# Two products between a snapshot and the next use of its bank, half of the output-weight casts on ScalarE, and three more weight sums in image 0

## The chip, the cores and the metric

The kernel runs on one core of a Trainium2 chip. The time is the device time of one execution in microseconds (us). The kernel before takes 420.86 us (median of 3 runs, 420.32 to 421.15). A result is called faster or slower when it differs by over 2%. Engines: TensorE (PE), VectorE (DVE), ScalarE (ACT), GpSimd (POOL); SyncE (SP) starts the transfers.

## The reference, cut to what matters

```python
# attention with a sigmoid, 8 images x 12 heads x 448 tokens x 64
scores = q @ k.T / 8 - log(448)
x = (1 / (1 + exp(-scores))) @ v            # -> 3584 x 768
# gated feed-forward layer, d_ff = 1536
out = (maximum(x @ w_gate, 0) * (x @ w_val)) @ w_out
```

## The kernel before: the parts that matter here

Each image has three attention blocks of four heads. While PE works on the feed-forward layer of image b, "visits" slip in attention work of image b+1: scores of two chunks on PE, their sigmoids on ACT, at the end of a block its values on PE. Image 0's layer uses plain products. From image 1 on a matrix product in two by two blocks is made of seven products instead of eight, which needs sums of weight blocks (T) and of input blocks (S).

A product adds into a bank of PSUM. Some banks are read half-way (the snapshot), and later products of the same bank may not start before that read is over:

```python
BANK = {1: "b1", 2: "b1", 6: "b2", 5: "b2", 3: "b2", 7: "b3", 4: "b3"}
# 1, 6 and 7 take a free bank (there are four); 2, 3 and 4 give theirs back
if k == 1:   nc.scalar.copy(tmp(key, "s1")[:], ps)                    # ACT snapshot, then 2 adds on
elif k == 6: add(tmp(key, "s2")[:], ps, live[key, "s1"][:])           # DVE snapshot, then 5 adds on
elif k == 5: add(t[:], ps, live[key, "s1"][:])                        # DVE snapshot, then 3 adds on
elif k == 2: nc.scalar.activation(tmp(key, "r1")[:], ps, AF.Relu); give(i)
elif k == 3: add(t[:], ps, t[:]); give(i); <POOL: hT = r1 * t>        # frees s1 for a later product 1
```

The order at the start of an image, (group, product); the next image's (0,1) is issued before the last two output products:

```python
todo += gv((0,7),(0,2),(0,6),(0,5),(1,1),(1,6),(0,3),(0,4),(1,5),(1,7),(1,2),(2,1),(1,3))
```

The loop of image 0, cut, with the weight sums on DVE (8 of 12; the other four follow in image 1). `due` and `wdue` are lists of planned times, `later` the blocks whose transposes are still to come:

```python
for step, cost in enumerate(ffn0()):
    t += cost
    ...                                     # loads; POOL casts all 12 tiles of w_out
    if due and t >= due[0]:
        due.pop(0); settle = t + 1.3; visit()
    if later and t >= settle:
        m = later.pop(0); transposes(m, "k"); transposes(m, "q")   # PE, then DVE copies kT, qT
    if wdue and t >= wdue[0]:
        wdue.pop(0); gv_weights(*wsums.pop(0))                     # one weight sum on DVE
```

Of the kernel before, what the change touches and what calls it, by code (L numbers as in the profile page):

```python
# [16 lines left out]
def kernel(  # L17
# [10 lines left out]
    nc = tc.nc  # L28

    B, H, S, D = q.shape  # L30
# [54 lines left out]
    NG = NFC // FG  # L85
# [3 lines left out]
    wo = wpool.tile([P, NFC, DM], FP16, name="wo")  # L89
    hT = wpool.tile([P, NFC, NHALF * S], FP16, name="hT")  # L90

    staged: dict = {}
    qk16: dict = {}
    keys16: dict = {}
# [64 lines left out]
    def load_cast_out(f: int, eng):  # L159

        st = stp.tile([P, 2, S], FP32, tag="st", name="st_wo")
        flat = st[:].rearrange("p r s -> p (r s)")[:, 0:DM]
        nc.sync.dma_start(flat, moe_w_out[f * P : (f + 1) * P, :])
        eng.tensor_copy(wo[:, f], flat)  # L164


    def dma_transposes(n: int):
# [138 lines left out]
    HFC = NFC // 2  # L306
# [4 lines left out]
    def subtract(out, a, b):  # L311
        nc.vector.tensor_tensor(out=out, in0=a, in1=b, op=AOP.subtract)
# [4 lines left out]
    def gv_weights(k: int, j: int):  # L317

        B11, B21 = wg[j][:, 0:HDC], wg[j][:, HDC:NDC]
        B12, B22 = wv[j][:, 0:HDC], wv[j][:, HDC:NDC]  # L320
        if k == 3:
            T[k, j] = B12
            subtract(B12, B12, B22)
            return
        i = 3 * j + (1, 2, 4).index(k)
        if i % 2 == 0:
            T["tile"] = swp.tile([P, 2, HDC, FG * P], FP16, tag="sw", name="Tw")
        T[k, j] = T["tile"][:, i % 2]
        a, b = {1: (B12, B11), 2: (B22, T.get((1, j))), 4: (B21, T.get((2, j)))}[k]
        subtract(T[k, j], a, b)  # L330
# [29 lines left out]
    def sums(what, ks):  # L360

        if what[0] == "x":
            xa, xb = xT[what[1], 0], xT[what[1], 1]
            A11, A21, A12, A22 = xa[:, :, 0:HS], xa[:, :, HS:S], xb[:, :, 0:HS], xb[:, :, HS:S]
            n, w = HDC, HS
        else:
            o = what[1] * P % (NHALF * S)
            A11, A12 = hT[:, 0:HFC, o : o + P], hT[:, HFC:NFC, o : o + P]
            o = (what[1] + 1) * P % (NHALF * S)
            A21, A22 = hT[:, 0:HFC, o : o + P], hT[:, HFC:NFC, o : o + P]  # L370
            n, w = HFC, P
        for k in ks:
            tile_ = sxp.tile([P, HFC * P], FP16, tag=f"S{k}", name=f"S{k}")
            t = tile_[:, 0 : n * w].rearrange("p (c s) -> p c s", c=n)
            if k == 3:
                subtract(t, A21, A11)
            elif k == 2:
                add(t, A22, S_[what, 3])
            elif k == 1:
                add(t, A21, A22)  # L380
            else:
                subtract(t, A12, S_[what, 2])
            S_[what, k] = t
# [170 lines left out]
    def ffn(b: int):  # L554


        p, o = 4 * (b - 1), 4 * (b - 1) + 2
        gv = lambda *gk: [("gv", b, *x) for x in gk]
        todo = gv((0, 1)) if b == 1 else []
        todo += gv((0, 7), (0, 2), (0, 6), (0, 5), (1, 1), (1, 6), (0, 3), (0, 4), (1, 5), (1, 7), (1, 2), (2, 1), (1, 3))  # L560
        for g in range(2, HFC):
            todo += gv((g, 6), (g - 1, 4), (g, 7), (g, 5), (g, 2))

            todo += gv((g + 1, 1)) if g + 1 < HFC else [("out", p if b > 1 else o, 1)]
            todo += gv((g, 3))
        todo += gv((HFC - 1, 4))
        behind = {("out", o, k): [] for k in (6, 5, 3)}
        end = ("gv", b, HFC - 1)
        nxt = [("gv", b + 1, 0, 1)] if b + 1 < B else []
        if b == 1:  # L570
            todo += ["plain"] + [("out", o, k) for k in (6, 2, 7, 5)] + nxt + [("out", o, k) for k in (3, 4)]
            behind[*end, 4] = [(("h", o), [3, 2, 1, 4])]
            behind["out", o, 5] = [(("x", 2), [3, 2, 1])]
        else:
            todo += [("out", p, k) for k in (7, 2, 6)] + [("out", o, 1), ("out", p, 5), ("out", o, 2), ("out", p, 3)]
            todo += [("out", o, 7), ("out", o, 6), ("out", p, 4), ("out", o, 5)] + nxt + [("out", o, 3), ("out", o, 4)]

            early = b < 5
            behind[*end, 5] = [(("h", p), [3, 2, 1] if early else [3])]
            behind[*end, 3] = [(("h", p), [4] if early else [2])]  # L580
            behind[*end, 4] = [] if early else [(("h", p), [1, 4])]
            behind["out", p, 6] = [(("h", o), [3])]
            behind["out", p, 5] = [(("h", o), [2])]
            behind["out", p, 3] = [(("h", o), [1, 4])]
            if nxt:
                behind["out", o, 6] += [(("x", b + 1), [3])]
                behind["out", o, 5] += [(("x", b + 1), [2, 1])]
        if nxt:
            behind["out", o, 3] += [(("x", b + 1), [4])]
        return todo, behind  # L590

    def one(x, behind):
        (gv_product if x[0] == "gv" else out_product)(*x[1:])
        for what in behind.get(x, []):
            sums(*what)
# [32 lines left out]
    visits = []  # L628
    for b in range(1, B):
# [3 lines left out]
        for i in range(n0 * NCH + 1, n1 * NCH, 2):  # L633
            n = i // NCH - 1
# [5 lines left out]
    def visit():  # L640
        todo = visits.pop(0)
        for what, i in todo:
            if what == "v":
                values(i, range(NCH))
            else:
                scores(*divmod(i, NCH))
        for what, i in todo:
            if what == "s":
                feed(i)

    def dues(first, last):

        work = [sum(1.2 if what == "v" else 1.0 for what, _ in x) for x in visits]
        at = [0.0]
        for x, w in zip(visits, work):
            if x[0][0] == "v":
                break
            at.append(at[-1] + w)
        return [first + a / at[-1] * (last - first) for a in at]
# [9 lines left out]
    with tc.manual_schedule():  # L669
# [47 lines left out]
        for i in range(NP0 + 2):  # L717
            n, c = divmod(i, NCH)
# [21 lines left out]
        total = (NFC * 2 * NDC - 7) * MM_US  # L740
        due = dues(3.0, total - 4.5)
        T0 = 11.5
        wsums = [(k, j) for j in range(NG - 1) for k in (1, 2, 4, 3)]
        wdue = [T0 + i * (total - 4.5 - T0) / len(wsums) for i in range(len(wsums))]
        xsums = [3, 2, 1, 4]
        t = 0.0
# [27 lines left out]
            start_next()  # L774


        late = [lambda k=k: gv_weights(k, NG - 1) for k in (1, 2, 3, 4)]
        late_out = [lambda k=k, part=part: out_weights(k, part) for k in (1, 2, 4) for part in range(2)]
        for b in range(1, B):
            todo, behind = ffn(b)  # L780
            plain_us = 2 * NFC * (DM / 2400.0 + 0.004)
            us = lambda x: plain_us if x == "plain" else GV_US if x[0] == "gv" else OUT_US
            total = sum(us(x) for x in todo)
            due = dues(1.5 if b > 1 else 2.0, total - 4.2) if b + 1 < B else []
            t = 0.0
            for x in todo:
                if x == "plain":
                    t1 = t
                    for block in range(2):
                        for cost in out_plain(block):  # L790
                            t1 += cost
                            if due and t1 >= due[0]:
                                due.pop(0)
                                visit()
                            if late_out and t1 - t >= (7 - len(late_out)) * 1.1:
                                late_out.pop(0)()
                    assert not late_out
                    out_weights(3, 0)
                else:
                    one(x, behind)  # L800
                t += us(x)
                if due and t >= due[0] and (x[0] == "out" or x[-1] in (2, 6, 7)):
                    due.pop(0)
                    visit()
                    if late:
                        late.pop(0)()
            assert not due and not late
        assert not visits and len(free) == 4
# [1 line left out]
_INS = ['q', 'k', 'v', 'moe_w_gate', 'moe_w_val', 'moe_w_out']  # L810
# [26 lines left out]
```

## Time and profile before

| | before |
|---|---|
| time, median | 420.86 us |
| span of the profiled run | 418.6 us |
| PE busy | 397.4 us, 95% |
| DVE, ACT, POOL busy | 68%, 57%, 40% |
| longest wait of PE | 2.84 us, at 80.5 to 83.3 us |
| period of images 3 to 6 | 49.75 us |

PE is the bound, so what counts is where PE stands still or runs at half clock (82.60 to 89.43 us, by the clock record). The prediction shows those lines; in a timeline line the columns are start, length, engine, line of the kernel, operation, output and inputs, shape, how many, and in brackets the idle time just before with what ended it.

### The profile page before, as it was taken

The page shows a single profiled execution, that of the slowest core. Times are in us where ns is not written, and L with a number is a line of the kernel's source. Part 1 is how long each engine was busy: PE and PEld are TensorE (multiplying, and loading weights), DVE is VectorE, ACT ScalarE, POOL GpSimd, SP SyncE. Part 2 cuts the span into 40 slices and gives each one's busy share as a digit, 9 for nine tenths or more (in the row PEclk, how much of TensorE's full clock was granted, in tenths as well). Part 3 has the DMA queues.
Part 4 walks back from the last instruction along what each step waited for, and adds up shares of the span by engine and source line. Part 5 has one row for each costly group of instructions (what it writes and reads, how often), then busy time and mean ns, then how long its engine had stood idle before and what let it go on. Part 6 is the DMA issues. An engine that isn't in the chain of part 4 may idle for free.

```text
span 418.6 us, 9648 instructions
## 1 busy us (share of the span) xinstructions
PE 397.4 (95%) x3946; PEld 276.6 (66%) x3946; DVE 284.7 (68%) x467; ACT 237.6 (57%) x332; POOL 167.0 (40%) x184
## 2 busy tenths in 40 slices
PE   7889999699998999999999999999999999999994
PEld 3335446578567875688757786577865787559962
DVE  3544877577968776576765677576766767658883
ACT  6957775347445675466845666547665567532220
POOL 2677956854413364053440645214540334002300
PEclk9999999979999999999999999999999999999999
DMA  8999959356087616476255854378362950041006
GB/s 300 383 384 385 369 135 402 127 158 171 2 252 184 196 56 172 112 216 177 47 169 124 182 165 117 115 144 182 125 177 76 193 106 2 2 113 39 2 2 150
DMA packets 64476, 67.08 MB, mean 160 GB/s; under 512 B 35888, under 2 KB 54832, under 8 KB 64432
## 3 DMA queue, kind: packets, MB, share of 16 engines
q1 hardware_dynamic: 63184, 64.53, 54.2%
q10 hardware_dynamic: 1248, 1.93, 1.3%
q8 instruction: 31, 0.51, 0.5%
q14 instruction: 13, 0.11, 0.1%
HBM read 47.19 MB, written 11.01 MB: 139 GB/s over the span
## 4 chain that ended last, share of the span: by engine, by line
PE 77%; DMA 9%; DVE 6%; POOL 3%; issue 1%; ACT 1%; SPq 1%; ACTq 0%; DVEq 0%
PE bank L400 57%; PE pair L196 8%; PE pair L225 7%; DMA st_wu<-in_moe_w_val_dram 3%; PE bank L263 3%; DMA st_wo<-in_moe_w_out_dram 3%; DMA st_k<-in_k_dram 2%; DVE s L315 2%; PE bank L538 2%; POOL wo L164 1%; DVE s L489 1%; DVE S L315 1%; POOL h16k L133 1%; ACT PT L206 1%; ACT r L442 1%
## 5 line engine op out<-in xcount | busy, mean ns | idle before, releaser
L206 ACT ACTIVATE PT<-pair,bias_t 128x896 f16<-128x896 f32 x168 | 160.9, 1014 | 54.1 <-PE pair L196 52.6
L315 DVE TENSOR_TENSOR s<-bank,s 128x448 f32<-128x448 f32 x210 | 127.1, 622 | 63.0 <-PE bank L400 48.6
L450 POOL TENSOR_TENSOR hT<-r,s 128x448 f16<-128x448 f32 x39 | 45.2, 1159 | 173.2 <-DVE s L315 108.8
L400 PEld LDWEIGHTS <-Tw 128*128 128x128 f16 x756 | 71.4, 98 | 18.5 <-issue 18.3
L400 PE MATMUL bank<-S,Tw 128*128 128x224 f16 x504 | 62.6, 260 | 8.4 <-DVE s L315 5.3
L400 PE MATMUL bank<-S,wv 128*128 128x224 f16 x504 | 62.1, 259 | 0.2 <-DVE s L315 0.2
L400 PE MATMUL bank<-xT,wg 128*128 128x224 f16 x504 | 60.3, 261 | 0.0
L196 PE MATMUL pair<-qT,kT 64*64 64x448 f16 x672 | 54.1, 366 | 5.0 <-ACT PT L206 3.4
L442 ACT ACTIVATE r<-bank 128x448 f32<-128x448 f32 x42 | 22.8, 543 | 54.9 <-PE bank L400 54.9
L400 PEld LDWEIGHTS <-wg 128*128 128x128 f16 x504 | 47.4, 99 | 7.4 <-issue 6.2
L400 PEld LDWEIGHTS <-wv 128*128 128x128 f16 x504 | 48.1, 98 | 2.4 <-issue 1.3
L400 PEld LDWEIGHTS <-S 128*128 128x128 f16 x312 | 29.1, 98 | 24.9 <-issue 7.8
L196 PEld LDWEIGHTS <-kT 64*64 64x64 f16 x672 | 17.6, 105 | 32.3 <-issue 26.6
L455 DVE SCALAR_TENSOR_TENSOR hT<-s,s 128x448 f16<-128x448 f32 x42 | 36.1, 860 | 1.4
L489 DVE SCALAR_TENSOR_TENSOR s<-bank,s 128x384 f32<-128x384 f32 x26 | 14.5, 557 | 30.2 <-PE bank L400 30.2
L225 PE MATMUL pair<-PT,v 64*64 64x448 f16 x588 | 32.9, 361 | 0.0
L133 POOL CAST h16q<-st_q 128x896 f16<-128x896 f32 x21 | 20.3, 968 | 30.5 <-DMA st_q<-in_q_dram 23.2
L400 PEld LDWEIGHTS <-hT 128*128 128x128 f16 x234 | 22.9, 98 | 14.2
L243 ACT ACTIVATE xT<-pair 128x448 f16<-128x448 f32 x42 | 20.5, 541 | 20.2 <-PE pair L225 19.4
L400 PE MATMUL bank<-xT,Tw 128*128 128x224 f16 x252 | 31.1, 260 | 0.0
L400 PE MATMUL bank<-wo,S 128*128 128x384 f16 x156 | 29.5, 326 | 1.1 <-DVE s L489 0.6
L400 PE MATMUL bank<-To,S 128*128 128x384 f16 x156 | 29.7, 327 | 0.3 <-DVE s L489 0.3
(68 smaller groups left out, 419.2 us busy)
## 6 DMA issues: line engine op xcount, KB each, us to landing
st_q<-in_q_dram SPq DMA_DIRECT2D x23, 448.0 KB, 4.6
st_v<-in_v_dram SPq DMA_DIRECT2D x23, 448.0 KB, 5.3
out_dram<-ysb SPq DMA_DIRECT2D x53, 192.0 KB, 2.7
st_k<-in_k_dram SPq DMA_DIRECT2D x22, 448.0 KB, 4.0
st_wg<-in_moe_w_gate_dram SPq DMA_DIRECT2D x6, 768.0 KB, 11.9
st_wu<-in_moe_w_val_dram SPq DMA_DIRECT2D x6, 768.0 KB, 12.3
st_wo<-in_moe_w_out_dram SPq DMA_DIRECT2D x12, 384.0 KB, 6.2
st_v<-in_v_dram ACTq DMA_DIRECT2D x1, 448.0 KB, 5.5
```

Source lines behind the costliest of these rows:

```text
L133: eng.tensor_copy(o, i)
L196: nc.tensor.matmul(ps[o : o + 64, bank, 0:S], kT[r : r + 64, c, h, :], qT[r : r + 64, :, h, :], start=True, stop=True, tile_position=(r, o ...
L206: nc.scalar.activation(pt[:], ps[:, :, 0:S], AF.Sigmoid, bias=bias_t[:], scale=qk_scale)
L225: nc.tensor.matmul(pv[pr][o : o + 64, 0:S], t[r : r + 64, pr, c * D : (c + 1) * D], pt[r : r + 64, pr, :], start=(c == 0), stop=(c == NCH ...
L243: nc.scalar.activation(x, pv[pr][:, 0:S], AF.Copy, scale=XSCALE)
L263: nc.tensor.matmul(banks[begun[key]][:, 0:S], w[j][:, dc, jj * P : (jj + 1) * P], xT[b, dc // 3][:, dc % 3], start=(dc == 0), stop=(dc == ...
L315: nc.vector.tensor_tensor(out=out, in0=a, in1=b, op=AOP.add)
L400: nc.tensor.matmul(bank[:, c0:c1], lhsT, rhs, start=(first and i == 0), stop=last, skip_group_check=True)
L442: nc.scalar.activation(tmp(key, "r1")[:], ps, AF.Relu)
L450: eng.tensor_tensor(out=out[:, :, o : o + HS], in0=two(live[key, "r1"]), in1=two(t), op=AOP.mult)
L455: nc.vector.scalar_tensor_tensor(out=out[:, :, o + HS : o + S], in0=two(t), scalar=0.0, in1=two(live[key, "s4"]), op0=AOP.max, op1=AOP.mult,)
L489: nc.vector.scalar_tensor_tensor(out=out, in0=ps, scalar=OUT_SCALE, in1=c, op0=AOP.mult, op1=AOP.add)
```

## The change

It has three intents: an order in which two products lie between a snapshot and the next use of its bank (also across the border of two images, and without a visit right ahead of a product 2, whose relu frees a bank; between the longer products of the output it is one in places); six of the twelve output-weight casts on ACT, so that POOL is free earlier; and three of the four late weight sums already in image 0.

```diff
-        eng.tensor_copy(wo[:, f], flat)
+        if f < HFC:
+            eng.tensor_copy(wo[:, f], flat)
+        else:
+            late_casts.append(lambda: nc.scalar.copy(wo[:, f], flat))
...
-        todo += gv((0, 7), (0, 2), (0, 6), (0, 5), (1, 1), (1, 6), (0, 3), (0, 4), (1, 5), (1, 7), (1, 2), (2, 1), (1, 3))
+        todo += gv((0, 7)) if b == 1 else []
+        todo += gv((0, 6), (0, 2), (1, 1), (0, 5), (1, 6), (1, 2), (0, 3), (1, 5), (0, 4), (1, 7), (2, 1), (1, 3))
...
-        nxt = [("gv", b + 1, 0, 1)] if b + 1 < B else []
+        nxt = [("gv", b + 1, 0, 1), ("gv", b + 1, 0, 7)] if b + 1 < B else []
...                                            # the sums of x and h behind the products move along
+                todo += [("out", o, 6), ("out", p, 4), ("out", o, 5), ("out", o, 7), ("out", o, 3), ("out", o, 4)]   # last image
...
-        wsums = [(k, j) for j in range(NG - 1) for k in (1, 2, 4, 3)]
+        wsums = [(k, j) for j in range(NG) for k in (1, 2, 4, 3)][:-1]
...
+                if late_casts and n >= 5 and n % 2:
+                    late_casts.pop(0)()
...
-                if due and t >= due[0] and (x[0] == "out" or x[-1] in (2, 6, 7)):
+                fits = x[0] == "out" or x[-1] in (6, 7) or (x[-1] == 2 and len(visits[0]) == 2 if visits else False)
+                if due and t >= due[0] and fits and not (nx and nx[0] == "gv" and nx[-1] == 2):
...
-                    if late:
-                        late.pop(0)()
+                    if (3, NG - 1) not in T:
+                        gv_weights(3, NG - 1)
```

More of the change, by code (lines that the diff above doesn't have):

```diff
@@ L90 @@
     hT = wpool.tile([P, NFC, NHALF * S], FP16, name="hT")
+    late_casts: list = []
     staged: dict = {}
@@ L572, in ffn @@
             behind[*end, 4] = [(("h", o), [3, 2, 1, 4])]
-            behind["out", o, 5] = [(("x", 2), [3, 2, 1])]
+            behind["out", o, 7] = [(("x", 2), [3])]
+            behind["out", o, 5] = [(("x", 2), [2, 1])]
         else:
             todo += [("out", p, k) for k in (7, 2, 6)] + [("out", o, 1), ("out", p, 5), ("out", o, 2), ("out", p, 3)]
-            todo += [("out", o, 7), ("out", o, 6), ("out", p, 4), ("out", o, 5)] + nxt + [("out", o, 3), ("out", o, 4)]
+            if nxt:
+                todo += [("out", o, 7), ("out", o, 6), ("out", p, 4), ("out", o, 5)] + nxt + [("out", o, 3), ("out", o, 4)]
+            else:
+                todo += [("out", o, 6), ("out", p, 4), ("out", o, 5), ("out", o, 7), ("out", o, 3), ("out", o, 4)]
             early = b < 5
@@ L580, in ffn @@
             behind[*end, 3] = [(("h", p), [4] if early else [2])]
-            behind[*end, 4] = [] if early else [(("h", p), [1, 4])]
-            behind["out", p, 6] = [(("h", o), [3])]
+            behind["out", p, 6] = [(("h", o), [3])] if early else [(("h", p), [1, 4]), (("h", o), [3])]
             behind["out", p, 5] = [(("h", o), [2])]
-            behind["out", p, 3] = [(("h", o), [1, 4])]
-            if nxt:
+            behind["out", p, 3] = [(("h", o), [1, 4] if nxt else [1])]
+            if not nxt:
+                behind["out", o, 6] = [(("h", o), [4])]
+            else:
                 behind["out", o, 6] += [(("x", b + 1), [3])]
@@ L774 @@
             start_next()
-        late = [lambda k=k: gv_weights(k, NG - 1) for k in (1, 2, 3, 4)]
         late_out = [lambda k=k, part=part: out_weights(k, part) for k in (1, 2, 4) for part in range(2)]
@@ L785 @@
             t = 0.0
-            for x in todo:
+            for n, x in enumerate(todo):
                 if x == "plain":
@@ L800 @@
                     one(x, behind)
+                if late_casts and n >= 5 and n % 2:
+                    late_casts.pop(0)()
                 t += us(x)
-                if due and t >= due[0] and (x[0] == "out" or x[-1] in (2, 6, 7)):
+                nx = todo[n + 1] if n + 1 < len(todo) else None
+                fits = x[0] == "out" or x[-1] in (6, 7) or (x[-1] == 2 and len(visits[0]) == 2 if visits else False)
+                if due and t >= due[0] and fits and not (nx and nx[0] == "gv" and nx[-1] == 2):
                     due.pop(0)
                     visit()
-                    if late:
-                        late.pop(0)()
-            assert not due and not late
+                    if (3, NG - 1) not in T:
+                        gv_weights(3, NG - 1)
+            assert not due
         assert not visits and len(free) == 4
```

## The prediction

> **What bounds the kernel now.** I read the page first, then the list of waits, then the timeline around each wait.
>
> ```profile
> PE 397.4 (95%) x3946; PEld 276.6 (66%) x3946; DVE 284.7 (68%) x467; ACT 237.6 (57%) x332; POOL 167.0 (40%) x184
> PEclk9999999979999999999999999999999999999999
> ```
>
> TensorE (PE) is busy 95% of the 418.6 us span; the next engine, VectorE (DVE), 68%. A change that adds or removes no matmul can win only PE's idle time and the dip in its clock (slice 9, near 85 us). In whose name PE waits:
>
> ```profile
> PE bank L400 <- DVE s L315: 5.5, 9, 2.8
> PE bank L400 <- ACT r L442: 2.6, 6, 0.5
> PE bank L400 <- DVE s L489: 0.9, 2, 0.6
> ```
>
> Line 400 is the seven-product scheme. A product is six matmuls, 0.575 us (start to start, 72.19 to 72.76; output products 0.975). A *snapshot* reads a half-accumulated bank before the next product may add to it. One of the nine DVE waits is 2.84 us long:
>
> ```profile
> 76.98 3.09 POOL L164 CAST wo<-st_wo 128x768 f16<-128x768 f32 x3
> 80.02 0.93 POOL L133 CAST h16k<-st_k 128x896 f16<-128x896 f32 x1
> 80.92 1.12 POOL L450 TENSOR_TENSOR hT<-r,s 128x448 f16<-128x448 f32 x1
> 82.07 0.53 ACT L435 COPY s<-bank 128x448 f32<-128x448 f32 x1 [4.14 <-POOL hT L450]
> 82.64 0.62 DVE L315 TENSOR_TENSOR s<-bank,s 128x448 f32<-128x448 f32 x1 [4.26 <-ACT s L435]
> 83.31 1.28 PE L400 MATMUL bank<-S,Tw 128*128 128x224 f16 x6 [2.84 <-DVE s L315]
> 79.00:91.00 12.00, 9.16 (x86) 6.00 (x79) 5.89 (x8) 5.92 (x9) 6.71 (x9) 0.72 0.58 153
> 91.00:103.00 12.00, 12.00 (x133) 10.37 (x132) 9.48 (x16) 6.99 (x11) 8.28 (x9) 1.00 0.57 156
> ```
>
> Read it backwards: PE waits for DVE's snapshot, that for ScalarE's (ACT) copy, that for a buffer that GpSimd's (POOL) gate multiply frees, and the multiply stands behind twelve casts of the output weights. Then the clock falls: 86 matmuls in 12 us against 133. The other waits are short and recur at the start of each image (period 49.75 us):
>
> ```profile
> 177.99 0.73 PE L400 MATMUL bank<-S,Tw 128*128 128x224 f16 x6 [0.28 <-DVE s L315]
> 184.93 0.73 PE L400 MATMUL bank<-S,Tw 128*128 128x224 f16 x6 [0.42 <-ACT r L442]
> 376.79 0.73 PE L400 MATMUL bank<-S,Tw 128*128 128x224 f16 x6 [0.79 <-DVE s L315]
> 411.93 1.14 PE L400 MATMUL bank<-wo,S 128*128 128x384 f16 x6 [0.65 <-DVE s L489]
> ```
>
> The first and third are product 6 followed at once by 5, the second a bank that ACT's relu frees late because two sigmoids stand before it, the fourth 5 followed at once by 3 in the last output pair. Idle time here leaves out the drain of the last matmul, so I take the loss from starts: the gap from a product's last matmul to the next product's first, less 0.096 us, or less 0.28 where sigmoid work lies between.
>
> [...] matmuls start every 0.2 us instead of 0.096 from 83.3, and full clock is back at 89.4. [...] one weight sum takes 0.95 us at 59.16 with POOL idle, 1.68 at 47.52 under casts. [...]
>
> **The change part by part.** I walked the issue loops of both versions by hand.
>
> *Start of image 1.* POOL's casts run from 66.06 at about 1.0 us each (8.02/8). With six of them POOL is through at 72.1 and the casts of q and k end near 74; the multiply that blocked is wanted near 74.5. The 2.84 us stall and the clock dip should go. From 67.58, where the products of line 400 begin, to the end of the 22nd (91.0) the work is 22 x 0.575 + 3 visits x 0.6 + 2.0 for the visit with values = 16.45 us, so it would end at 84.0: before loses 7.0 us. (A visit is a slot of attention work between products.) New losses: the six casts, [...] go to ACT at products 6, 8, 10, 12, 14 and 16, among eight sigmoids of 1.0. Following ACT's queue, three places stall PE: product (1,2), three after (1,1), whose copy stands behind two sigmoids, 0.9; the visit after (2,6), whose pair is not yet free, 0.4; and (3,6), whose bank the late relu frees, 0.9. Sum 2.2. Gain 7.0 - 2.2 = 4.8.
>
> *Weight sums in image 0.* Eleven instead of eight in the same stretch, so sum (4,0) moves ahead of the transpose copies of block 5. There PE already waits for DVE, which has been busy without a gap since 44.34:
>
> ```profile
> 47.52 1.68 DVE L312 TENSOR_TENSOR Tw<-wv,Tw 128x1536 f16<-128x1536 f16 x1
> 49.13 0.61 DVE L187 COPY kT<-bank 128x896 f16<-128x896 f16 x1
> 50.32 0.38 PE L196 MATMUL pair<-qT,kT 64*64 64x448 f16 x4 [0.54 <-DVE qT L187]
> ```
>
> One more sum in front makes that wait longer by its own 1.15 to 1.7 us: cost 1.4. Later DVE has 5 us of slack (58 to 66), so the other sums should cost nothing. The sums taken out of image 1 delayed no product there: gain 0.
>
> *Image starts 3 to 6 (four).* Per start, from the gaps: 0.24 (output 5, one product, output 3, at 172.8), 0.35 (6 to 5) and 0.58 (bank behind relu) = 1.17. All three get two products or an earlier relu: 4 x 1.17 = 4.7. In the new order I find no new wait: the snapshot of (0,6) is done about 0.2 us before (0,5) would start.
>
> *Start of image 2.* Losses 0.24 + 0.68 + 0.35 + 0.64 = 1.9, some because two sums of x ran at 1.05 to 1.23 us under POOL's casts. As (0,6) now follows the last output product at once, a bank wait may stay: gain 1.2.
>
> *Last image.* Start: 0.24 + 0.95 + 0.32 = 1.5. End: 0.81 for 5 to 3, now with one 0.975 us product between, less 0 to 0.1; and 0.46 at 403.7, where product 5 now waits for its sum instead of the snapshot, gain 0.1 to 0.2. Together 2.4.
>
> Sum: -4.8 + 1.4 - 4.7 - 1.2 - 2.4 = -11.7 us. 420.9 - 11.7 = 409.2; I say 409.
>
> **Rivals.** *(a) ACT becomes the bound of image 1's start.* For: the casts sit in ACT's strict queue and the loads behind them landed late before (the ninth at 75.3), so a cast that waits for its transfer would hold sigmoids and copies. Against: image 0 now ends later, and ACT should reach the third late cast near 76.7, after the landing. If it happens, a further 1 to 3 us, and if the clock dips again 3 more: 410 to 414. *(b) DVE becomes the bound of image 0.* For: 8 sums fill most of 44 to 58 already and POOL casts make each 70% longer. Against: four banks let PE run two hidden slices ahead of a late multiply, and the slack after 58 exceeds the three new sums (3 x 0.95). If so, 2 to 3 us more: 411 to 412. *(c) The short waits only move.* Two products, 1.15 us, between snapshot and reuse leave little over 0.2 + 0.62 us of drain and add if DVE has anything queued. Should half come back, 4 us are lost: 413. *(d) It goes better:* late casts hide wholly and the extra sum costs 1.15 or less: 406 to 407.
>
> **Range and chances.** The periodic part (4.7 + 1.5 + most of the end) is measured several times over; image 1's start is the uncertain term (2 to 6.5), image 0 next (0.5 to 3). That gives 405.5 to 413. The 2% line is 412.4; it needs a loss of 3.4 us on my sum, so (a) with a dip or (b) and (c) together: faster 0.83, within 2% 0.16, slower 0.01.
>
> **What would show it.** Right: no clock below full near 85 us; "ACT s L435 <- POOL hT L450" gone or small; POOL's output casts six in one run, [...] the wait for DVE's qT copy near 50 us grown to about 1.7 to 2.2; image period 48.6 instead of 49.75 us; product 6 to 5 without a wait. Wrong: new waits of PE on sigmoids or on ACT's snapshot copies over 3 us in 68 to 90, ACT copies waiting for DMA, or a period that stays above 49.3.

## The result, and the profile after

The changed kernel takes 408.35 us (median of 4 runs, 407.36 to 409.65); the kernel before on the same chip 420.74. The ratio is 0.9707 with a 95% interval of 0.967 to 0.9745. Ratios here are the mean time of one kernel's fast runs over that of the other's fast runs of the same rounds, so not quite the ratio of the medians. All runs told here are of the fast state. The prediction, 409.0 in 405.5 to 413, holds; its terms do not all hold.

First the page of the changed kernel (busy time of the engines; TensorE's granted clock in 40 slices) and its list of PE's waits (total us, times, longest). Its line numbers are 4 higher than before in this part of the code: line 404 holds the products, 200 the scores.

```profile
PE 393.9 (97%) x3946; PEld 276.4 (68%) x3946; DVE 280.5 (69%) x467; ACT 242.9 (60%) x338; POOL 158.4 (39%) x178
PEclk9999989999999999999999999999999999999998
```

```profile
PE pair L200 <- ACT PT L210: 3.2, 9, 0.7
PE pair L200 <- DVE qT L191: 2.5, 2, 2.3
...
PE bank L404 <- ACT s L439: 0.5, 1, 0.5
```

The waits of the products for DVE (5.5 us before) and for the relu (2.6 us before) are gone from the top, and so is the clock dip at slice 9. In their place there is one wait of 2.3 us for DVE's qT copy, and a new dip in slice 6.

To see where the time went, I cut both traces at moments that have the same PE work ahead of them: the start of the values of each image's last block (block 5, 8, 11 and so on; for the first cut block 3).

| stretch | before | after | change | predicted |
|---|---|---|---|---|
| up to block 3's values | 39.84 | 40.24 | +0.40 | 0 |
| image 0 (to block 5's values) | 21.74 | 24.89 | +3.15 | +1.4 |
| image 1 | 57.86 | 51.99 | -5.87 | -4.8 |
| image 2 | 50.48 | 48.78 | -1.70 | -1.2 |
| images 3 to 6, each | 49.75 | 48.45 | -1.30 (x4 = -5.20) | -1.17 (x4 = -4.7) |
| last image, to the last matmul's start | 44.80 | 42.93 | -1.87 | -2.4 |
| rest of the span | 4.92 | 5.24 | +0.32 | 0 |
| span | 418.64 | 407.87 | -10.77 | -11.7 |

At each cut the same number of matmuls lies behind in both traces. The 0.40 us of the first row are spread: all kernels have the same code up to there, and apart from one trace with an early clock dip they reach that cut at 39.84 to 40.35 us.

The start of image 3 after, PE and ACT. Before, product 6 to 5 waited here (177.99) and a product behind the late relu (184.93):

```profile
171.63 0.74 PE L404 MATMUL bank<-S,Tw 128*128 128x224 f16 x6
172.20 1.31 PE L404 MATMUL bank<-xT,wg 128*128 128x224 f16 x12
173.35 1.31 PE L404 MATMUL bank<-S,Tw 128*128 128x224 f16 x12
175.28 0.54 ACT L446 ACTIVATE r<-bank 128x448 f32<-128x448 f32 x1 [1.15 <-PE bank L404]
175.72 1.90 ACT L210 ACTIVATE PT<-pair,bias_t 128x896 f16<-128x896 f32 x2
```

Two products (172.20) lie between 6 (171.63) and 5 (173.35), and the relu at 175.28 stands ahead of the sigmoids. From 165 to 360 us the list of PE's waits is empty.

The timeline of image 0 after, DVE and PE:

```profile
49.31 2.04 DVE L316 TENSOR_TENSOR Tw<-wg,Tw 128x1536 f16<-128x1536 f16 x1
51.81 0.61 DVE L191 COPY qT<-bank 128x896 f16<-128x896 f16 x1
52.47 0.38 PE L200 MATMUL pair<-qT,kT 64*64 64x448 f16 x4 [2.29 <-DVE qT L191]
53.18 1.85 PE L267 MATMUL bank<-xT,wg 128*128 128x448 f16 x6
```

Sum (4,0) now stands ahead of the copy and takes 2.04 us, while POOL is casting. PE waits 2.29 us instead of 0.54. Then six plain matmuls take 1.85 us where they took 1.30: the clock record of this trace has half clock from 53.78 to 57.20, that is 3.41 us.

The start of image 1 after, POOL, ACT and PE:

```profile
69.97 3.77 POOL L166 CAST wo<-st_wo 128x768 f16<-128x768 f32 x4 [0.15 <-DMA st_wo<-in_moe_w_out_dram]
78.57 1.14 POOL L454 TENSOR_TENSOR hT<-r,s 128x448 f16<-128x448 f32 x1 [2.28 <-ACT wo L168]
75.85 0.54 ACT L439 COPY s<-bank 128x448 f32<-128x448 f32 x1
77.66 2.29 ACT L168 CAST wo<-st_wo 128x768 f16<-128x768 f32 x3
76.45 0.73 PE L404 MATMUL bank<-xT,wg 128*128 128x224 f16 x6 [0.52 <-ACT s L439]
```

POOL's gate multiply no longer stands behind casts: POOL is idle for 2.28 us before it (the bracket names a cast, which only ended last; the multiply needs DVE's sum of product 3, done at 78.41). No product waits for it, and PE keeps full clock. What is left is the 0.52 us wait of product (1,2) for ACT's copy of (1,1). Counted from starts, as the prediction counts, it is 0.68 us, where the prediction has 0.9.

The last image after, PE, at the two places that lost most before:

```profile
365.24 0.74 PE L404 MATMUL bank<-S,Tw 128*128 128x224 f16 x6
365.81 1.31 PE L404 MATMUL bank<-xT,wg 128*128 128x224 f16 x12
366.96 1.31 PE L404 MATMUL bank<-S,Tw 128*128 128x224 f16 x12
...
399.85 2.11 PE L404 MATMUL bank<-wo,S 128*128 128x384 f16 x12
```

Product 6 starts at 365.24, (0,2) and (1,1) follow, then 5 and (1,6) from 366.96, none with a bracket: no idle time. At 399.85 product 7 and then 3 of the output run as one piece.

### The profile page after: what moved, and what is told of

It is laid out like the page before. It is cut to its first block, busy times and chain, and to the rows that moved or that the text cites. A ratio compares the mean times of both kernels' runs of the same rounds, so it can differ in the third digit from the quotient of the medians.

```text
span 407.9 us, 9655 instructions
## 1 busy us (share of the span) xinstructions
PE 393.9 (97%) x3946; PEld 276.4 (68%) x3946; DVE 280.5 (69%) x467; ACT 242.9 (60%) x338; POOL 158.4 (39%) x178
## 4 chain that ended last, share of the span: by engine, by line
PE 83%; DVE 2%; ACT 1%; issue 1%; ACTq 0%; DVEq 0%
PE bank L404 62%; PE pair L200 8%; PE pair L229 7%; PE bank L267 3%; PE bank L542 2%; ACT PT L210 1%; DVE Tw L316 1%; DVE S L319 1%; DVE s L319 0%; ACT r L446 0%; DVE ysb L493 0%; DVE s L493 0%; ACT s L439 0%; DVE qT L191 0%; DVE kT L191 0%
## 5 line engine op out<-in xcount | busy, mean ns | idle before, releaser
L404 PE MATMUL bank<-S,Tw 128*128 128x224 f16 x504 | 60.9, 259 | 0.5 <-DVE s L319 0.2
L404 PE MATMUL bank<-xT,wg 128*128 128x224 f16 x504 | 58.7, 259 | 0.5 <-ACT s L439 0.5
L459 DVE SCALAR_TENSOR_TENSOR hT<-s,s 128x448 f16<-128x448 f32 x42 | 30.1, 716 | 1.4
L404 PE MATMUL bank<-wo,hT 128*128 128x384 f16 x156 | 29.7, 326 | 0.0
```

Of the source, the lines that this page charges most:

```text
L404: nc.tensor.matmul(bank[:, c0:c1], lhsT, rhs, start=(first and i == 0), stop=last, skip_group_check=True)
L459: nc.vector.scalar_tensor_tensor(out=out[:, :, o + HS : o + S], in0=two(t), scalar=0.0, in1=two(live[key, "s4"]), op0=AOP.max, op1=AOP.mult,)
```

## The experiments

My theory after this result: the order earns its gain on its own; the casts and the sums both remove the same stall of image 1, so their gains do not add; and the sums cost in image 0 what the table shows, through one wait and a clock dip that follows from it. The main rivals: the parts add up, or image 1 had to be rid of the sums for ACT and DVE to keep up.

### One part at a time

Three kernels with one part each, and one with all but the sums, ran on one chip, 3 rounds.

**Only the sums.**

```diff
-        wsums = [(k, j) for j in range(NG - 1) for k in (1, 2, 4, 3)]
+        wsums = [(k, j) for j in range(NG) for k in (1, 2, 4, 3)][:-1]
-        late = [lambda k=k: gv_weights(k, NG - 1) for k in (1, 2, 3, 4)]
+        late = [lambda: gv_weights(3, NG - 1)]
```

> The kernel before with only the weight sums moved (eleven in image 0, one left for image 1). Theory, the parts interact: image 0 gets longer by about 3.1 us as in the changed kernel (a wait of 2.3 us for the qT copy near 50 us instead of 0.5, then a short clock dip), but the chain of output-weight casts on GpSimd does not shift with it, so the 2.84 us stall and the clock dip near 83 us, together with their followers about 6 us, mostly go: 417 to 419 us, a ratio of 0.990 to 0.997. Rival, the parts add up: image 1 keeps its stall and the run takes about 424 us, ratio 1.007.

Measured: 419.69 us (median of 20 runs), before 420.05, ratio 0.9987 (0.9974 to 1.0). This lies between the two expectations, nearer to the theory's: the addition rival is out, but the gain is smaller than I said. In the trace, which shows one of the quicker runs (417.93 us, no dip at all), image 0 is 1.63 us longer than before and image 1 4.5 us shorter (53.32 for 57.86); PE waits 2.2 us for qT. The other 19 runs took 417.5 to 421.4, all with a mean clock below its 1.0 (0.989 to 0.999); where their dips lie, some of them perhaps behind the last matmul, the times alone do not tell. Why the stall is gone the trace shows:

```profile
80.23 1.13 POOL L450 TENSOR_TENSOR hT<-r,s 128x448 f16<-128x448 f32 x1
81.40 0.53 ACT L435 COPY s<-bank 128x448 f32<-128x448 f32 x1 [1.23 <-POOL hT L450]
```

POOL's gate multiply comes 0.7 us earlier than before (80.92), but PE's products of image 1 begin 2.07 us later (69.64 for 67.58), so ACT's copy waits 1.23 us instead of 4.14.

**Only the casts.**

```diff
+        if f < HFC:
             eng.tensor_copy(wo[:, f], flat)
+        else:
+            late_casts.append(lambda: nc.scalar.copy(wo[:, f], flat))
...
+                if late_casts and n >= 5 and n % 2:
+                    late_casts.pop(0)()
```

> The kernel before with only half of the output-weight casts moved to ScalarE. Theory: the GpSimd multiply no longer stands behind twelve casts, the 2.84 us stall and the clock dip go (7 us lost there before), ScalarE casts that wait for their landing give 2 to 4 us back: 415.5 to 418.5 us, ratio 0.988 to 0.995, and full clock from 60 to 100 us. Rival, ScalarE becomes the bound of the start of image 1: at least as slow as before, ratio 1.000 or more, with waits of PE for the sigmoid or for ScalarE's snapshot copy over 5 us in 66 to 92.

Measured: 415.67 us, ratio 0.9885 (0.9861 to 0.9908), by the 2% rule the same, but clear of noise; full clock in all slices. The stall is gone and image 1 takes 53.14 us, 4.7 less. PE's waits in image 1 come to 1.7 us, the longest 0.9 for a relu on ACT. The theory holds, and ACT does not become the bound.

**Only the order** (the changed kernel with both other parts undone).

```diff
-        if f < HFC:
-            eng.tensor_copy(wo[:, f], flat)
-        else:
-            late_casts.append(lambda: nc.scalar.copy(wo[:, f], flat))
+        eng.tensor_copy(wo[:, f], flat)
-        wsums = [(k, j) for j in range(NG) for k in (1, 2, 4, 3)][:-1]
+        wsums = [(k, j) for j in range(NG - 1) for k in (1, 2, 4, 3)]
...                                                # `late` back as before
```

> The changed kernel with all twelve output casts back on GpSimd and the weight sums back as before, so only the order of the products (and of the visits and sums that follow it). Theory: the starts of images 2 to 6 and the last image win what the traces show in the changed kernel (1.7 + 5.2 + 1.6 = 8.5 us), image 1 keeps a stall of 2.5 to 3.5 us behind GpSimd's casts and its clock dip: 411 to 413 us, ratio 0.977 to 0.982. Rival, most of the gain of the change is the removed stall of image 1: ratio above 0.987.

Measured: 411.49 us, ratio 0.9782 (0.9766 to 0.9799). As the theory says, images 3 to 6 take 48.45 us each, and image 1 keeps its stall. It is even longer (PE's timeline; lines 401 and 316 of this kernel are 404 and 319 of the changed one):

```profile
84.37 1.28 PE L401 MATMUL bank<-S,Tw 128*128 128x224 f16 x6 [4.51 <-DVE s L316]
```

With it and the dip (1.28 us for six matmuls that take 0.74 before it) image 1 takes 59.11 us, 1.25 more than before. So the order alone brings three quarters of the gain. In percent of before, the parts alone bring 0.1 (sums), 1.15 (casts) and 2.2 (order), together 3.5; the whole, on another chip, brings 2.9. Most of what is missing is the stall, which can be removed only once: the sums gain 4.5 us in image 1 alone, but 1.45 us there when the casts and the order are changed too, as the next kernel shows.

**All but the sums.**

```diff
-        wsums = [(k, j) for j in range(NG) for k in (1, 2, 4, 3)][:-1]
+        wsums = [(k, j) for j in range(NG - 1) for k in (1, 2, 4, 3)]
...
+                    if late:
+                        late.pop(0)()
...                                                # `late` back as before
```

> The changed kernel with the weight sums as in before (eight in image 0, four in image 1). Theory, the sums in image 0 cost 3.1 us (1.75 of wait, 1.4 of half clock) and image 1 has room for them: image 0 back to before's length, of which image 1 gives back 0 to 1.5 us since its casts now come earlier against their landing: 405.5 to 407.5 us, ratio 0.963 to 0.968. Rival, the sums had to leave image 1: ratio 0.971 or more, with new waits of PE for VectorE's snapshots in 66 to 92.

Measured: 407.16 us, ratio 0.9683 (0.9669 to 0.9698); the runs lie within 0.9 us of each other. The time is in the theory's range, the ratio just outside. Image 0 is back at 21.75 us, 3.1 less than in the changed kernel's profiled run, but image 1 takes 53.44 instead of 51.99, the upper end of what I gave for it. The rival's sign shows too, but small: PE waits 0.8 us for DVE's snapshots in image 1. Two of these waits (0.46 and 0.15) end behind DVE work that a late sum holds up (79.86 to 81.27). So where image 0 dips, the sums there cost about 3.1 us and image 1 returns nearly half of it. Against the changed kernel's 0.9707 and 0.974, from other chips, this is ahead by 0.2 to 0.6%.

### The wait in image 0, and the clock

The next four kernels ran on another chip, 5 rounds.

**The changed kernel again.**

> The changed kernel unchanged, to see the spread of its runs. Theory: whether the 2.3 us wait in image 0 drops the clock is a matter of chance, so the runs fall in two groups about 2 us apart (the first four were 407.36, 407.37, 409.32 and 409.65 us with mean clocks 0.998, 0.999, 0.996 and 0.993), and the longer ones have the lower clock. Rival: one group with a spread under 1 us. Ratio 0.968 to 0.973 either way.

Measured: 408.29, 409.78, 409.82 and 409.83 us, with mean clocks 1.000, 0.996, 0.995, 0.996; median 409.8, ratio 0.974 (0.9718 to 0.9761). Two groups again, 1.5 us apart here, though more runs fell into the slower one and the ratio came out a little above what I gave. The profiled run is of the slower group, and its clock record has half clock from 53.24 to 56.66 us, 3.41 us again.

**The wait filled.** Ten matmuls stand ahead of the scores that wait for qT; their result is never read.

```diff
         for what, i in todo:
+            if what == "s" and i == (NPRO - 1) * NCH:
+                warm_bank = take()
+                for _ in range(10):
+                    nc.tensor.matmul(banks[warm_bank][:, 0:512], wg[0][:, 0, 0:P], wg[0][:, 0, 0:512], start=True, stop=True)
+                give(warm_bank)
             if what == "v":
                 values(i, range(NCH))
```

> The changed kernel with ten idle-time matmuls (512 columns, to a free bank, never read) put before the scores that wait for the qT copy, so that PE works through the 2.3 us wait. Theory: the wait stays, the clock never drops, and all runs lie near the faster group of the changed kernel: 406.8 to 408, spread under 1 us, ratio 0.967 to 0.970, image 0 about 23.4 us long instead of 24.9. Rival, the time after the wait is lost to something else than the clock (VectorE's backlog): times and image 0 as in the profiled run of the changed kernel, about 409.5 us in half of the runs.

Measured: 408.23 us, ratio 0.9725 (0.9702 to 0.9749); four runs at 408.03 to 408.72, one at 410.19 with a mean clock of 0.996. PE's timeline:

```profile
50.22 2.33 PE L656 MATMUL bank<-wg 128*128 128x512 f16 x10
52.49 0.38 PE L200 MATMUL pair<-qT,kT 64*64 64x448 f16 x4
53.19 1.30 PE L267 MATMUL bank<-xT,wg 128*128 128x448 f16 x6
```

The scores start at the same moment as in the changed kernel (52.49, 52.47), so the wait is all there. But the six plain matmuls behind it take 1.30 us again, not 1.85, and image 0 takes 23.39 us instead of 24.89. So the 1.5 us after the wait are the clock and not DVE's backlog. The one long run shows that some dip can still happen; only one run of each kernel has a trace, so where it was is open. Time and ratio came out a little above the ranges that I gave, and with the long run counted the interval overlaps that of the changed kernel: the traces carry this verdict, not the ratios. Image 1 takes 51.99 us here as in the changed kernel, though it starts 1.4 us earlier.

What decides whether the clock falls at a wait of about this length is not shown. The traces have both cases. Before, PE stands from 80.47 to 83.31 us and the clock falls at 82.60, for 6.83 us. In the changed kernel PE waits for 2.29 us, up to 52.47, and the clock falls at 53.78, 1.3 us after the wait's end, for 3.41 us. In the sums alone PE waits 2.2 us for the same copy, and that run's mean clock is 1.0. By the mean clocks the changed kernel had the dip in 5 of its 8 runs.

**The sums held back until the copies are through.**

```diff
-            if wdue and t >= wdue[0]:
+            if wdue and t >= wdue[0] and not later:
```

> The changed kernel with the weight sums held back while block 5's transposes are still to come, so that its kT and qT copies stand ahead of sum (4,0). Theory: the wait for qT goes back to about 0.5 us, no clock dip can follow, image 0 is 21.7 to 22.3 us long instead of 24.9, image 1 stays within 1 us of 52.0: 404.5 to 406.5 us, ratio 0.961 to 0.966, ahead of the changed kernel by 2 to 3 us. Rival, VectorE has too much to do in image 0 whatever the order: the wait only moves to a later bank and the ratio stays at 0.969 or more.

Measured: 406.57 us, ratio 0.967 (0.9651 to 0.9689), 0.7% ahead of the changed kernel in the same rounds. Image 0 takes 21.56 us and the wait for qT is short (first line, PE); the mean clocks of the four runs are 0.998 and 0.999. VectorE has the time for eleven sums in image 0; only their place was wrong. But the ratio is at the edge of what I gave, because image 1 takes 53.39 us and not 52.0. The second line (ACT) says why:

```profile
50.14 0.38 PE L200 MATMUL pair<-qT,kT 64*64 64x448 f16 x4 [0.35 <-DVE qT L191]
...
73.86 0.83 ACT L168 CAST wo<-st_wo 128x768 f16<-128x768 f32 x1 [1.20 <-DMA st_wo<-in_moe_w_out_dram]
```

Image 1 now starts 3.7 us earlier (67.39 for 71.13), and ACT reaches its first late cast before the weights have landed. Everything behind it on ACT is late; PE waits 0.8 us for sigmoids and 0.7 for a copy and a relu. This is the prediction's rival (a). The changed kernel escapes it because its image 0 ends later, which is the reason that the prediction gave against (a).

**And the first visit later,** after (1,2) instead of before (1,1).

```diff
-   ... and not (nx and nx[0] == "gv" and nx[-1] == 2):
+   ... and not (nx and nx[0] == "gv" and nx[-1] == 2) and not (b == 1 and n == 3):
```

> The same, and the first visit of image 1 moved from before product (1,1) to after (1,2), so that ScalarE's copy of (1,1) no longer stands behind two sigmoids. Theory: the 0.52 us wait for ScalarE's copy near 76 us goes, 0.4 to 0.8 us less than with the sums held back alone: 404 to 406 us. Rival: the later visit crowds the sigmoids against the late casts and the wait returns at the next pair of banks: no difference, or slower by up to 1 us.

Measured: 407.76 us, ratio 0.9702 (0.9685 to 0.9719), 1.2 us longer than without it. The 0.5 us wait for the copy is gone, but PE waits 1.9 us for sigmoids. The rival holds, a little beyond the bad end of its range.

### The late casts spread, and the end of the last image

A last call on a third chip, 5 rounds.

**The casts spread out.**

```diff
-                if late_casts and n >= 5 and n % 2:
+                if late_casts and n in (8, 17, 19, 24, 26, 30):
```

> The kernel with the sums held back, and the six late casts spread over products 9, 18, 20, 25, 27 and 31 instead of 6, 8, 10, 12, 14 and 16. Theory: with image 0 short again ScalarE reached the first late cast before its transfer had landed (1.2 us of wait) and then ran behind, so that image 1 took 53.4 us instead of 52.0; spread out, the casts wait for nothing and the waits of PE for sigmoids in 66 to 92 (0.8 us) go: image 1 at 51.5 to 52.3 us, 404.4 to 405.8 us, 0.2 to 0.5% ahead of the sums held back alone. Rival, image 1 is longer for another reason (GpSimd or VectorE nearer to it): no difference.

Measured: 405.81 us, ratio 0.9652 (0.963 to 0.9675). Image 1 takes 51.77 us, and the waits for sigmoids at its start are gone. The profiled run is the slowest of the four (406.97; the others 405.04 to 406.06): it has a clock dip of 3.41 us near 10 us, before any of the changed parts, and reaches block 3's values at 41.67 us instead of near 40. The theory holds for image 1; the gain over the sums held back alone is 0.2% in the ratio, from different chips, within both intervals.

**And the later visit with them.**

> The spread casts and the first visit of image 1 after (1,2). Theory: now that no cast crowds ScalarE the later visit wins what it lost before, the 0.5 us wait for the copy of (1,1): 0.3 to 0.7 us less than the spread casts alone. Rival: the later visit lacks time before the next one whatever the casts do: no difference.

Measured: 404.86 us (404.65 to 405.26 in five runs), ratio 0.9628 (0.961 to 0.9646). Image 1 takes 51.10 us, 0.67 less than with the spread casts alone, as the theory says (the medians differ by 0.95, but one of the four runs of the spread casts is known to hold a dip). PE has no wait in 60 to 92 us. The same edit that lost 0.6 us in that stretch when ACT was crowded (53.99 for 53.39) wins when it is not. This kernel beats both: 3.7% under before, and by the ratios to before (0.9707 and 0.974 on other chips) 0.8 to 1.1% under the changed kernel.

**The old end of the last image.**

```diff
-            if nxt:
-                todo += [("out", o, 7), ("out", o, 6), ("out", p, 4), ("out", o, 5)] + nxt + [("out", o, 3), ("out", o, 4)]
-            else:
-                todo += [("out", o, 6), ("out", p, 4), ("out", o, 5), ("out", o, 7), ("out", o, 3), ("out", o, 4)]
+            todo += [("out", o, 7), ("out", o, 6), ("out", p, 4), ("out", o, 5)] + nxt + [("out", o, 3), ("out", o, 4)]
```

> The changed kernel with the output products of the last image in the order of before (7 before 6, product 3 at once after 5). Theory: the wait of product 3 for VectorE's snapshot of 5 comes back: 0.7 to 0.9 us longer than the changed kernel, ratio higher by about 0.002, PE waits 0.6 us for L493 before its last but one product. Rival: the tail is set by the stores, no difference in the end.

Measured: 409.1 us, ratio 0.9727 (0.9703 to 0.9751), which can't be told from the changed kernel's 0.9707 and 0.974: the two groups of clock (mean clocks of 0.994 and 0.996, 0.998 and 0.999) cover so small a difference. The trace tells more. PE's timeline has the wait back:

```profile
401.22 1.14 PE L404 MATMUL bank<-wo,S 128*128 128x384 f16 x6 [0.65 <-DVE s L493]
```

The last image, to the last matmul's start, takes 43.71 us instead of 42.93, 0.78 more. The stores behind it end 5.02 us after that instead of 5.24, so about 0.2 of it is given back. The theory holds in the trace; in the time it stays unproven.

## Why the prediction was right, point by point

- **The bound.** PE stays the bound: it is busy 97% of the span after.
- **Start of image 1: right in mechanism and near in size.** POOL's casts, ACT's copy, DVE's snapshot and PE hung together as read, and taking six casts off POOL removes stall and dip (the casts alone do it). I had 2.2 us of new losses; the changed kernel has 0.9: counted from starts, 0.68 at (1,2) and 0.2 near (3,6), and nothing at the visit after (2,6). The longer image 0 is not the reason: with the wait filled, image 0 takes 23.39 us, 0.25 more than I said, and image 1 takes the same 51.99. Why my walk of ACT's queue by hand gave too much at the visit and at (3,6) stays open. When image 0 is as short as before, the losses do appear where I listed them: (1,2), the visit after (2,6) and (3,6) have brackets of 0.51, 0.32 and 0.52 (its two chunks), and 0.19 us, and image 1 takes 2.3 us more than the 51.10 that it takes without waits.
- **Weight sums in image 0: the mis-sized term.** The prediction says that the wait grows "by its own 1.15 to 1.7 us: cost 1.4". The place was right, and the sum there took 2.04 us, so the wait grew by 1.75 (2.29 less 0.54). I took the casts for a slowdown of 70%. The single records show a wait instead: the sum starts at 49.31, a cast that had begun before it ends at 50.55, and the sum ends 0.80 us after that; before, at 47.52, it is 0.81 us after the cast's end. In these two traces a 128x1536 fp16 sum takes 0.94 to 0.96 us with no POOL instruction beside it or when it starts ahead of one (at 70.90 before, where the cast beside it takes 1.62 us, and one at 75.33 takes 0.83), and up to 2.18 us when a cast has started first. What the step left out besides is that the clock can fall after a wait of that length, as it does at 53.78 us: another 1.4 us (3.15 less 1.75) when it does, in 2 of the first 4 runs and 3 of the second 4, if the mean clock is taken as the sign. I had read the 2.84 us case a few lines above and did not apply it, and I read it a little wrong: by the clock record the clock falls at 82.60, 2.13 us into that wait and not at its end. The dip lasts 6.83 us there and 3.41 us in the changed kernel.
- **"The other sums should cost nothing"**: right. With only their place changed, image 0 is as short as before. **"The sums taken out of image 1 ... gain 0"**: not quite. With four late sums image 1 takes 53.44 us instead of 51.99, and 0.6 us of its waits end behind a late sum on DVE. But with the sums held back, where no late sums are left but one, it takes 53.39, with other waits (for sigmoids). So the earlier start of image 1 costs something too, and how much falls to each stays open.
- **Images 3 to 6: right,** 1.30 us each for 1.17 predicted, and the order alone gives it. No new wait shows in these stretches.
- **Image 2: right,** -1.7 for -1.2. Of the bank wait that I feared, 0.17 us is left.
- **Last image: right in mechanism, a little too large:** -1.9 for -2.4, and the tail gives 0.3 back. At its start a wait of 0.18 us is left, a snapshot that stands behind another on DVE, and near its end one of 0.21 for a sum (393.99), which the prediction expected.
- **New ACT casts:** 0.82 to 0.88 us each in the traces, 0.84 on average in the changed kernel. No trace of before has one of this size, so the length that the prediction's walk of ACT's queue used was not shown.
- **The rivals.** (a) does not happen in the changed kernel and does happen in the better one; (b) and (c) do not happen. Against (a) the prediction held that image 0 ends later, and this is right: with an image 0 of 21.56 us (a) happens, with one of 23.39 it does not. What it did not see is that the delay which it counted as a cost keeps ACT from waiting, so that taking the delay away gains less than its length.

Two errors of 1 to 2 us, image 0 too short and image 1 too long, went in opposite directions, which is luck. The total fits better than its terms, and it fits the two slower runs (409.3 and 409.65) better than the two without the dip (407.4).

## What to carry to other kernels

When two parts of a change remove the same wait, measure each alone before adding their gains; here they sum to 3.5% and bring 2.9%. Before an extra operation is put on an engine that is not the bound, look at who waits for what stands behind it at that place: moving one sum behind two copies was worth more than all the sums' move. And price a wait of PE of some two microseconds, as they are here, at its own length plus a stretch at half clock that may follow (3.41 us in both profiled runs of the changed kernel).
